# Linear attention in rounds of two pairs of chunks: both projections side by side, the transposes of one pair at the end of the round

## The chip, the cores and the metric

The kernel runs on one core of one Trainium2 chip. The metric is the device time of one execution in microseconds (us), from start to end. A core has five engines: TensorE (PE; its weight loads are listed apart as PEld), VectorE (DVE), ScalarE (ACT), GpSimd (POOL) and SyncE (SP). Each runs its own instructions in order, and waits by semaphores for the others and for transfers. PSUM, the memory that matmuls write, has eight banks; a tile below is one or two of them.

## The reference

Two layers follow one another. The first is linear attention for 8 batches, 8 heads, 576 tokens and 64 numbers per head; the second sends each of the 4608 tokens through one of eight experts.

```python
def phi(x):
    proj = x @ w_phi                                  # 64 -> 128 features
    proj = proj - max(abs(proj), axis=-1)
    return concat([exp(proj), exp(-proj)])            # 256 features
q_p, k_p = phi(q), phi(k)
kv  = einsum('bhsf,bhsd->bhfd', k_p, v)               # a sum over the 576 tokens
z   = k_p.sum(over tokens)
num = einsum('bhsf,bhfd->bhsd', q_p, kv)
den = einsum('bhsf,bhf->bhs', q_p, z) + 1e-06
x   = num / den                                       # 512 numbers per token over all heads
# second layer, per token
logits = x @ w_gate; local = sigmoid(x @ w_local)
e = argmax(logits) if s == 0 or local < 0.5 else the previous token's e
out = softmax(logits)[e] * (relu(x @ w1[e]) @ w2[e])
```

Everything is float32. The change concerns the first layer alone.

## The kernel before

**Units, chunks, pairs.** Two batches and two heads form a unit; there are 4 x 4 = 16 units. The 1152 tokens of the two batches are cut into nine chunks of 128, so chunk 4 holds the end of one batch and the start of the other. The 144 chunks are handled in 72 pairs. A unit has two halves: chunks 0 to 4 (the first batch) and 4 to 8 (the second), each with a sum of its own.

**What is done with a pair**, with the lines of the profile:
- *projections* (`proj`, L183): 8 matmuls, which the profile counts as 16 weight loads, into the tile "pj" (two banks; there are two such tiles). DVE reduces to the largest absolute value (m, L186) and subtracts (sb, L188). ACT takes exp of the keys, with both signs (kp, L192).
- *transposes* (`qtr`, L203): four, of the queries' part of sb, into "qt", a single bank. ACT takes exp out of it (qp, L206).
- *sums* (`kv`, L225): 8 matmuls a chunk (16 for chunk 4, which belongs to both halves) gather the sum over tokens of features by values in "kvp", a single bank. When a half is complete, ACT copies it out twice (kf and kvs, L244 and L245).
- *turn* (L251): one step after that, kf is transposed into one of the two banks named "nm", and ACT copies it out (ks, L254). *Gate logits* (L263): one step later still, ks times the router's weights goes to the end of the other "nm" bank, and ACT copies it into kvs (L265). From then on the half's outputs stand in a list, `todo`.
- *outputs* (L284): 8 entries of `todo` a chunk, one matmul (two weight loads) each, in groups of two or three chunks, into an "nm" bank. The first group of a half uses the bank in which its gate logits were formed; the second group takes the next bank of the two. At a group's end DVE reads it in four instructions: den + 1e-06 and its reciprocal (rc, L301, L302), the output (xo, L306) and the logits (lg, L308). Only then is the bank free.

**The steps.** `step(p)` issues on PE the projections of pair p, the transposes of pair p-1, turns and gates that are due, the sums of the two chunks of pair p-2 (KVLAG = 2) up to the end of a half, up to 18 entries of `todo` (QUOTA), the rest of the sums, and then the router's chores. PE's order is exactly as it is written; the order on DVE, ACT, POOL and SP is made by a scheduler from the dependences. Inputs are fetched in groups of three chunks, a few pairs ahead.

**The router's chores.** When four units with the same two batches are done, a generator (`gate`) finds each token's expert from the logits, ranks the tokens and writes lists. It advances by up to six yields a step. Its small matmuls (L432, L442, L455, L466) use the "qt" bank under the name "pt". Three of the four such gates run beside the attention. Some chores are paced by POOL: `paced` copies the latest m.

After the attention, from about 340 us on, the experts run; each weight is split into a high and a low part and each product is three matmuls (L799 to L801). That part isn't changed.

Of the kernel before, what the change touches and what calls it, by code (L numbers as in the profile page):

```python
# [6 lines left out]
F32 = mybir.dt.float32  # L7
# [22 lines left out]
WE, WR, WL = 8, 4, 1  # L30
FILL = 6
KVLAG = 2
QUOTA = 18

# [12 lines left out]
class Kernel:  # L47
# [9 lines left out]
    def run(self):  # L57
        nc, tc, A = self.nc, self.tc, self.A
        act, dve = self.act, self.dve
        with ExitStack() as root:  # L60
# [35 lines left out]
            self.scattering = False  # L96
            self.tail, self.eslots, self.scattered = False, [], []
            self.g, self.ch, self.kvb, self.lg = {}, {}, {}, {}
            n = NBP * NHP * NC
# [7 lines left out]
            with tc.manual_schedule(engines={mybir.EngineType.PE}):  # L107
                for p in range(n // 2):
                    while self.fetched < n // 3 and self.fetched * 3 < 2 * p + 8:
                        self.fetch_kqv(self.fetched)  # L110
                    if p == FILL:
# [3 lines left out]
                    self.step(p, n)  # L115
            self.tail = True
            p = n // 2
            while p < n // 2 + KVLAG + 1 or self.todo or self.turns or self.gates:
                self.step(p, n)
                p += 1  # L120
            for x in self.background:
# [5 lines left out]
            more = lambda: next(plan, None)  # L127
# [44 lines left out]
    def proj(self, p):  # L172
# [3 lines left out]
        t = self.psf.tile([128, 2, 2, 2, 128], F32, name="pj")  # L176
        for i in (2 * p, 2 * p + 1):
            kq = self.g[i // 3]["kq"]
            s = slice(i % 3 * 128, i % 3 * 128 + 128)
            for j in (0, 1):  # L180
                for h in (0, 1):
                    r = slice(64 * h, 64 * h + 64)
                    self.last_pe = self.pe.matmul(t[:, h, i % 2, j, :], kq[r, j, s], self.w2[r], start=True, stop=True)  # L183
        m = self.m = self.front3.tile([128, 8], F32, name="m")
        f = t.rearrange("p h c j f -> p (h c j) f")
# [161 lines left out]

    def step(self, p, n):

        if p < n // 2:  # L350
            self.proj(p)
        if 0 <= p - 1 < n // 2:
            self.qtr(p - 1)
        gates, self.gates = self.gates, []
        turns, self.turns = self.turns, []
        for x in turns:
            x()
        for x in gates:
            x()
        parts = [[]]  # L360
        if 0 <= p - KVLAG < n // 2:
            for i in (2 * (p - KVLAG), 2 * (p - KVLAG) + 1):
                a, *more = self.kv(i)
                parts[-1] += a
                parts += more
        for x in parts[0]:
            x()
        for _ in range(min(QUOTA, len(self.todo)) if p < n // 2 else len(self.todo)):
            self.todo.pop(0)()
        for part in parts[1:]:  # L370
            for x in part:
                x()
        for x in list(self.background):
            for _ in range(6):
                y = next(x, self)
                if y is self:
                    self.background.remove(x)
                if y is self or y is STEP:
                    break

    def paced(self):

# [4 lines left out]
        return self.tc.issue_after(self.pool.tensor_copy(t, self.m[:, 0:1]).ins)  # L387

# [619 lines left out]
```

## Time and profile before

| | us |
|---|---|
| three runs | 838.76, 828.74, 834.18 |
| median | 834.18 |
| profiled execution | 827.13 |
| its span | 825.4 |
| mean granted clock of PE | 0.995 |

The profiled execution is the fastest of the times shown; around its span lie 1.7 us. Busy shares of the engines over the span say little about one stage, since the attention (up to some 335 us) and the experts have different limits. So the stage is read by its own windows and by PE's weight loads in order of time. In those rows stand start, length, engine, line, operation, output and inputs, and a count; behind them in brackets idle time and what ended it. The shape before the type is that of the tile which is read.

### The profile page before, as it was taken

The page shows a single profiled execution, that of the slowest core. Times are in us where ns is not written, and L with a number is a line of the kernel's source. Part 1 is how long each engine was busy: PE and PEld are TensorE (multiplying, and loading weights), DVE is VectorE, ACT ScalarE, POOL GpSimd, SP SyncE. Part 2 cuts the span into 40 slices and gives each one's busy share as a digit, 9 for nine tenths or more (in the row PEclk, how much of TensorE's full clock was granted, in tenths as well). Part 3 has the DMA queues.
Part 4 walks back from the last instruction along what each step waited for, and adds up shares of the span by engine and source line. Part 5 has one row for each costly group of instructions (what it writes and reads, how often), then busy time and mean ns, then how long its engine had stood idle before and what let it go on. Part 6 is the DMA issues. An engine that isn't in the chain of part 4 may idle for free.

```text
span 825.4 us, 23470 instructions
## 1 busy us (share of the span) xinstructions
PE 788.1 (95%) x9777; PEld 710.0 (86%) x9777; DVE 555.4 (67%) x956; ACT 428.2 (52%) x738; POOL 146.7 (18%) x156
## 2 busy tenths in 40 slices
PE   6999998999989899888999999999999999999997
PEld 5899987898878788777898998998898898999896
DVE  5677897679878885848754444644686777568541
ACT  4666665566666565323543333533564557447431
POOL 0000002200231132051421202212122212201010
PEclk9999999999999999999999999999999999999999
DMA  6545546764799531574974433744696687767510
GB/s 193 141 123 135 144 130 92 124 149 126 151 215 236 168 102 36 157 138 136 393 255 141 162 116 121 286 141 148 207 346 211 209 319 263 257 224 273 192 44 23
DMA packets 74239, 145.01 MB, mean 176 GB/s; under 512 B 9198, under 2 KB 48757, under 8 KB 74112
## 3 DMA queue, kind: packets, MB, share of 16 engines
q1 hardware_dynamic: 66272, 123.14, 50.9%
q0 software_dynamic: 7792, 20.02, 7.2%
q8 instruction: 79, 1.29, 0.7%
q10 hardware_dynamic: 64, 0.30, 0.1%
q14 instruction: 32, 0.26, 0.1%
HBM read 124.51 MB, written 20.26 MB: 175 GB/s over the span
## 4 chain that ended last, share of the span: by engine, by line
PE 69%; issue 12%; DMA 7%; DVE 6%; ACT 2%; POOL 2%; another core or an unknown queue 1%; SPq 1%; POOLq 0%; DVEq 0%; ACTq 0%
PE l L799 12%; PE l L800 12%; PE l L801 12%; PE kvp L225 8%; PE pj L183 8%; PE nm L284 8%; PE qt L203 4%; DMA out<-y,p_tokm 4%; DMA wraw<-in_w2h 2%; PE tr L791 1%; DVE sb L188 1%; DVE m L186 1%; PE nm L263 1%; POOL out L874 1%; DMA p_lrm<-lst,p_rim 1%
## 5 line engine op out<-in xcount | busy, mean ns | idle before, releaser
L753 ACT CAST whi<-wraw 128x1024 fp32r<-128x1024 f32 x160 | 167.5, 1048 | 205.7 <-PE l L801 111.6
L754 DVE TENSOR_TENSOR wlo<-wraw,whi 128x1024 fp32r<-128x1024 f32 x160 | 195.7, 1224 | 85.9 <-ACT whi L753 83.6
L799 PE MATMUL l<-xhi,whi 128*128 128x256 f32 x544 | 155.2, 286 | 2.1 <-DVE hl L822 1.4
L800 PE MATMUL l<-xlo,whi 128*128 128x256 f32 x544 | 152.8, 281 | 0.3 <-DVE xlo L794 0.3
L801 PE MATMUL l<-xhi,wlo 128*128 128x256 f32 x544 | 152.4, 280 | 0.0
L799 PE MATMUL l<-whi,hh 128*128 128x512 f32 x320 | 127.4, 398 | 0.7 <-DVE y L873 0.7
L800 PE MATMUL l<-wlo,hh 128*128 128x512 f32 x320 | 125.8, 393 | 0.0
L801 PE MATMUL l<-whi,hl 128*128 128x512 f32 x320 | 125.7, 393 | 0.0
L186 DVE TENSOR_REDUCE m<-pj 128x8 f32<-128x1024 f32 x72 | 87.9, 1220 | 43.9 <-PE pj L183 43.7
L206 ACT ACTIVATE qp<-qt 128x512 f32<-128x512 f32 x144 | 84.7, 604 | 60.3 <-PE qt L203 57.9
L192 ACT ACTIVATE kp<-sb 128x512 f32<-128x512 f32 x144 | 82.9, 623 | 54.2 <-DVE sb L188 46.5
L799 PEld LDWEIGHTS l<-xhi,whi 128*128 128x128 f32 x544 | 102.8, 189 | 4.5 <-DVE hl L822 1.9
L800 PEld LDWEIGHTS l<-xlo,whi 128*128 128x128 f32 x544 | 102.8, 189 | 1.1 <-DVE xlo L794 0.5
L801 PEld LDWEIGHTS l<-xhi,wlo 128*128 128x128 f32 x544 | 102.9, 189 | 0.0
L284 PE MATMUL nm<-kvs,qp 128*64 128x74 f32 x2304 | 89.0, 230 | 6.8 <-ACT kvs L265 4.8
L183 PE MATMUL pj<-first,kq 64*128 64x128 f32 x1152 | 86.9, 291 | 8.1 <-DMA kq<-in_kqT 6.4
L874 POOL DMA_INDIRECT out<-y,p_tokm x34 | 44.4, 1305 | 269.2 <-DVE y L873 250.7
L188 DVE TENSOR_TENSOR sb<-pj,m 128x1024 f32<-128x1024 f32 x72 | 88.1, 1224 | 3.7
L284 PEld LDWEIGHTS nm<-kvs,qp 128*64 128x64 f32 x2304 | 81.2, 139 | 8.1 <-ACT kvs L265 5.3
L183 PEld LDWEIGHTS pj<-first,kq 64*128 64x128 f32 x1152 | 72.6, 193 | 13.9 <-issue 6.8
L225 PE MATMUL kvp<-v,kp 128*64 128x65 f32 x2048 | 78.1, 227 | 0.5 <-ACT kvs L245 0.4
L225 PEld LDWEIGHTS kvp<-v,kp 128*64 128x64 f32 x2048 | 68.5, 140 | 6.6 <-issue 5.4
(200 smaller groups left out, 1000.3 us busy)
## 6 DMA issues: line engine op xcount, KB each, us to landing
wraw<-in_w1h SPq DMA_DIRECT2D x80, 512.0 KB, 5.9
wraw<-in_w2h SPq DMA_DIRECT2D x80, 512.0 KB, 4.4
kq<-in_kqT SPq DMA_DIRECT2D x47, 384.0 KB, 4.6
v<-in_va SPq DMA_DIRECT2D x48, 195.0 KB, 3.0
xs<-xo SPq DMA_DIRECT2D x48, 128.0 KB, 4.1
xs<-xo SPq DMA_DIRECT2D x16, 192.0 KB, 2.1
vs<-in_va SPq DMA_DIRECT2D x32, 32.5 KB, 3.0
lst<-pr,ri POOLq DMA_INDIRECT x36, 6.3
```

The costliest lines, as they stand in the source:

```text
L183: self.last_pe = self.pe.matmul(t[:, h, i % 2, j, :], kq[r, j, s], self.w2[r], start=True, stop=True)
L186: dve.tensor_reduce(m, f, AX.X, ALU.max, apply_absolute_value=True)
L188: self.last_dve = dve.tensor_sub(sb.rearrange("p h c j f -> p (h c j) f"), f, m.unsqueeze(2).broadcast_to([128, 8, 128]))
L192: self.last_act = act.activation(kp[:, :, :, sg, :].rearrange("p c h f -> p h c f"), sb[:, :, :, 0], AF.Exp, scale=1.0 - 2 * sg)
L206: self.act.activation(qp[:, sg], t, AF.Exp, scale=1.0 - 2 * sg)
L225: self.pe.matmul(self.kvp[r, sg, h], self.ch[i]["kp"][:, h, sg, r], self.v(i, b)[:, h], start=first and n < 2, stop=last and n >= 6)
L284: self.pe.matmul(e["t"][r, c - c0, h, :], self.ch[i]["qp"][:, sg, h, q0 + r.start:q0 + r.stop], kvs[:, sg, h, :], start=sg == 0, stop=sg == 1)
L753: self.act.copy(hi, raw)
L754: self.dve.tensor_sub(lo, raw, hi.bitcast(F32))
L799: mm(o, ah, bh, start=first, stop=False)
L800: mm(o, ah, bl, start=False, stop=False)
L801: self.last_pe = mm(o, al, bh, start=False, stop=last)
```

## The change

The work is cut into 36 rounds of two pairs instead of 72 steps of one. Round i issues on PE:
1. the projections of pairs 2i and 2i+1, one behind the other;
2. the transposes of pair 2i-1;
3. turns and gates that are due, now counted in rounds: a turn one round after its half is complete, and the gate one round after that;
4. the sums of chunks 4i-4 to 4i-1 up to the end of a half, up to 32 entries of `todo` (before 18 a step, so 36 in two), and the rest of the sums;
5. half of the router's chores;
6. the transposes of pair 2i;
7. the other half of the chores.

Before, two steps held projections, transposes and outputs twice each in turn. The chores keep two advances per two pairs. kp gets five buffers instead of four. m of both pairs is kept for the pacing. The input groups are fetched as far ahead of the round's second pair as before.

```diff
-FILL = 6
-KVLAG = 2
-QUOTA = 18
+FILL = 3
+QUOTA = 32
...
-                for p in range(n // 2):
-                    while self.fetched < n // 3 and self.fetched * 3 < 2 * p + 8:
+                for i in range(n // 4):
+                    while self.fetched < n // 3 and self.fetched * 3 < 4 * i + 10:
                         self.fetch_kqv(self.fetched)
...
-            while p < n // 2 + KVLAG + 1 or self.todo or self.turns or self.gates:
+            while i < n // 4 + 2 or self.todo or self.turns or self.gates:
...
-        kp = self.front3.tile([128, 2, 2, 2, 128], F32, name="kp", bufs=4)
+        kp = self.front3.tile([128, 2, 2, 2, 128], F32, name="kp", bufs=5)
...
-    def step(self, p, n):
-
-        if p < n // 2:
-            self.proj(p)
-        if 0 <= p - 1 < n // 2:
-            self.qtr(p - 1)
+    def step(self, i, n):
+
+        last = n // 2
+        for p in (2 * i, 2 * i + 1):
+            if p < last:
+                self.proj(p)
+        if 0 <= 2 * i - 1 < last:
+            self.qtr(2 * i - 1)
         gates, self.gates = self.gates, []
         turns, self.turns = self.turns, []
...
         parts = [[]]
-        if 0 <= p - KVLAG < n // 2:
-            for i in (2 * (p - KVLAG), 2 * (p - KVLAG) + 1):
-                a, *more = self.kv(i)
+        for c in range(4 * i - 4, 4 * i):
+            if 0 <= c < n:
+                a, *more = self.kv(c)
                 parts[-1] += a
                 parts += more
         for x in parts[0]:
             x()
-        for _ in range(min(QUOTA, len(self.todo)) if p < n // 2 else len(self.todo)):
+        for _ in range(min(QUOTA, len(self.todo)) if i < n // 4 else len(self.todo)):
             self.todo.pop(0)()
         for part in parts[1:]:
             for x in part:
                 x()
+        self.chores(0)
+        if 2 * i < last:
+            self.qtr(2 * i)
+        self.chores(1)
+
+    def chores(self, k):
+        self.half = k
         for x in list(self.background):
```

The lines of the changed kernel are one lower than before from L183 to L308 (L284 becomes L283, L308 becomes L307) and eight higher from the chores on.

How the change moves instructions is shown at three places. In the rows, the number behind a name tells one tile of that name from another, and a semaphore that an instruction waits for is in brackets.

**PE, where outputs change from one group to the next.** Before, in a step with a turn (nm_1446), the group nm_1371 is finished and nm_1477 is begun:

```order
L203 MATMUL qt_1438<-first_62,sb_1358 128x128 x3
L251 MATMUL nm_1446<-first_62,kf_1393 128x128 [waits DVE_49,PE_49,Activation_49]
L251 MATMUL nm_1446<-first_62,kf_1393 128x128
L225 MATMUL kvp_1451<-v_1040,kp_1285 64x65 [waits DMAHW2_49,Activation_49]
L225 MATMUL kvp_1451<-v_1040,kp_1285 64x65 x15
L284 MATMUL nm_1371<-kvs_1238,qp_1063 64x74 x2
L284 MATMUL nm_1477<-kvs_1238,qp_1063 64x74 [waits Activation_49]
L284 MATMUL nm_1477<-kvs_1238,qp_1063 64x74 x7
L284 MATMUL nm_1477<-kvs_1238,qp_1146 64x74 x8
```

The new group takes the bank of the turn, which ACT's copy frees. Now, in round 10, turn and gate (nm_1414) stand in one round, and the group nm_1273 is finished behind four chunks of sums:

```order
L262 MATMUL nm_1414<-wgi_68,ks_1271 64x18 [waits Activation_49]
L262 MATMUL nm_1414<-wgi_68,ks_1271 64x18 x3
L224 MATMUL kvp_1420<-v_919,kp_1241 64x65 [waits DMAHW0_49]
L224 MATMUL kvp_1420<-v_919,kp_1241 64x65 x15
L224 MATMUL kvp_1420<-v_919,kp_1257 64x65 x8
L224 MATMUL kvp_1420<-v_1065,kp_1257 64x65 [waits DMAHW2_49]
L224 MATMUL kvp_1420<-v_1065,kp_1257 64x65 x7
L283 MATMUL nm_1273<-kvs_997,qp_914 64x74 x8
L283 MATMUL nm_1468<-kvs_997,qp_914 64x74 [waits DVE_49,PE_49]
L283 MATMUL nm_1468<-kvs_997,qp_914 64x74 x7
L283 MATMUL nm_1468<-kvs_997,qp_958 64x74 x8
L283 MATMUL nm_1414<-kvs_1153,qp_958 64x74 [waits Activation_49]
```

The gate has the bank of the turn, and the group nm_1468 takes that of nm_1273, so its first output waits for DVE.

**DVE, at the same two places.** Before, the four instructions on the finished group nm_1371 stand behind reduce and subtract of the step's one pair:

```order
L186 TENSOR_REDUCE m_1431<-pj_1422 128x8 [waits PE_49]
L188 TENSOR_TENSOR sb_1433<-pj_1422,m_1431 128x1024 [waits DVE_49,Activation_49]
L301 TENSOR_SCALAR rc_1470<-nm_1371 128x4 [waits PE_49,Activation_49]
L302 RECIPROCAL rc_1470<-rc_1470 128x4 [waits DVE_49]
L306 TENSOR_TENSOR xo_1473<-nm_1371,rc_1470 128x256 [waits DMAHW6_49,DVE_49]
L308 TENSOR_TENSOR lg_430<-nm_1371,rc_1470 128x2x2x9
```

Now those on nm_1273 stand behind reduce and subtract of both pairs of round 10:

```order
L185 TENSOR_REDUCE m_1378<-pj_1369 128x8 [waits PE_49]
L187 TENSOR_TENSOR sb_1380<-pj_1369,m_1378 128x1024 [waits DVE_49,Activation_49]
L185 TENSOR_REDUCE m_1394<-pj_1385 128x8 [waits PE_49]
L187 TENSOR_TENSOR sb_1396<-pj_1385,m_1394 128x1024 [waits DVE_49,Activation_49]
L300 TENSOR_SCALAR rc_1461<-nm_1273 128x6 [waits PE_49]
L301 RECIPROCAL rc_1461<-rc_1461 128x6 [waits DVE_49]
L305 TENSOR_TENSOR xo_1464<-nm_1273,rc_1461 128x384 [waits DMAHW4_49,DVE_49]
L307 TENSOR_TENSOR lg_554<-nm_1273,rc_1461 128x3x2x9
```

Two more large instructions stand ahead of them within the round.

**ACT, at the end of a half.** Before, the two copies out of the sums' bank (kf_1393, kvs_1394) stand ahead of the exponentials of the keys of that step:

```order
L265 COPY kvs_1238<-nm_1371 128x4x9
L206 ACTIVATE qp_1368<-qt_1363 128x512
L244 COPY kf_1393<-kvp_1259 128x256
L245 COPY kvs_1394<-kvp_1259 128x4x65
L192 ACTIVATE kp_1360<-sb_1358 128x2x2x128 x2
L206 ACTIVATE qp_1443<-qt_1438 128x512
```

Now, in round 16, the second copy (kvs_2414) stands behind the exponentials of the first pair (kp_2351) and one of those of the second (kp_2367):

```order
L253 COPY ks_2381<-nm_2378 128x256
L191 ACTIVATE kp_2351<-sb_2349 128x2x2x128
L264 COPY kvs_2039<-nm_2383 128x4x9
L191 ACTIVATE kp_2351<-sb_2349 128x2x2x128
L243 COPY kf_2413<-kvp_2269 128x256
L205 ACTIVATE qp_2375<-qt_2370 128x512
L191 ACTIVATE kp_2367<-sb_2365 128x2x2x128
L244 COPY kvs_2414<-kvp_2269 128x4x65
L191 ACTIVATE kp_2367<-sb_2365 128x2x2x128
```

The copy has moved behind work on the round's second pair.

More of the change, by code (lines that the diff above doesn't have):

```diff
@@ L96, in run @@
             self.scattering = False
-            self.tail, self.eslots, self.scattered = False, [], []
+            self.tail, self.eslots, self.scattered, self.m = False, [], [], [None, None]
             self.g, self.ch, self.kvb, self.lg = {}, {}, {}, {}
@@ L386, in paced @@
         t = self.small.tile([128, 1], F32, name="tick", bufs=2)
-        return self.tc.issue_after(self.pool.tensor_copy(t, self.m[:, 0:1]).ins)
+        return self.tc.issue_after(self.pool.tensor_copy(t, self.m[self.half][:, 0:1]).ins)
     def pst(self, shape):
```

12 lines of the change are left out of this document (6 added, 6 removed).

## Prediction

> **What bounds the kernel now.** I read the page first: the busy rows, the chain of waits by engine, and the costliest groups.
>
> ```profile
> span 825.4 us, 23470 instructions
> PE 788.1 (95%) x9777; PEld 710.0 (86%) x9777; DVE 555.4 (67%) x956; ACT 428.2 (52%) x738; POOL 146.7 (18%) x156
> PE 69%; issue 12%; DMA 7%; DVE 6%; ACT 2%; POOL 2%; another core or an unknown queue 1%; SPq 1%; POOLq 0%; DVEq 0%; ACTq 0%
> L186 DVE TENSOR_REDUCE m<-pj 128x8 f32<-128x1024 f32 x72 | 87.9, 1220 | 43.9 <-PE pj L183 43.7
> L188 DVE TENSOR_TENSOR sb<-pj,m 128x1024 f32<-128x1024 f32 x72 | 88.1, 1224 | 3.7
> L183 PEld LDWEIGHTS pj<-first,kq 64*128 64x128 f32 x1152 | 72.6, 193 | 13.9 <-issue 6.8
> ```
>
> PE ends the kernel nearly alone, so an edit is worth what it takes from or adds to PE's row of work. The change touches only the attention stage, so I read it by windows next (us; busy and count of PE, PEld, DVE, ACT, POOL; granted clock).
>
> ```profile
> 50.00:100.00 50.00, 50.00 (x1126) 45.34 (x1122) 38.53 (x69) 31.44 (x70) 0.00 (x0) 1.00 0.48 131
> 250.00:300.00 50.00, 46.12 (x996) 41.47 (x992) 42.64 (x101) 30.99 (x64) 9.28 (x14) 0.99 0.72 194
> ```
>
> Between 50 and 100 us PE has no gap at all, while DVE is busy 38.53 of 50, 77%. Whatever makes PE wait is lost in full. Later, with the router's work beside it, PE is idle for 3.9 of 50 us.
>
> Then I read the weight loads on PE in order of time, since their starts give the pitch of the steps (start, length, instruction):
>
> ```profile
> 34.76 0.97 PEld L183 LDWEIGHTS pj<-first,kq 64*128 64x128 f32 x16
> ...
> 37.60 1.23 PEld L284 LDWEIGHTS nm<-kvs,qp 128*64 128x64 f32 x36
> 38.75 0.56 PEld L225 LDWEIGHTS kvp<-vs,kp 128*64 128x64 f32 x16
> ...
> 54.64 1.23 PEld L284 LDWEIGHTS nm<-kvs,qp 128*64 128x64 f32 x36
> 55.95 0.97 PEld L183 LDWEIGHTS pj<-first,kq 64*128 64x128 f32 x16
> 57.04 0.42 PEld L203 LDWEIGHTS qt<-first,sb 128*128 128x128 f32 x4
> 57.63 0.55 PEld L225 LDWEIGHTS kvp<-vs,kp 128*64 128x64 f32 x16 [0.17 <-issue]
> ...
> 59.42 0.55 PEld L225 LDWEIGHTS kvp<-vs,kp 128*64 128x64 f32 x16
> 59.88 0.55 PEld L225 LDWEIGHTS kvp<-v,kp 128*64 128x64 f32 x16
> ...
> 94.20 0.42 PEld L203 LDWEIGHTS qt<-first,sb 128*128 128x128 f32 x4
> ...
> 321.82 0.42 PEld L203 LDWEIGHTS qt<-first,sb 128*128 128x128 f32 x4
> ```
>
> From the transposes at 57.04 to those at 94.20 stand 9 undisturbed steps: 37.16 us, 4.13 each. 34.76 is where the projections of pair 8 start (the first of what will be round 4) and 321.82 where the transposes of the last pair stand: 287.1 us for 64 steps. At the undisturbed pitch they would take 64/9 x 37.16 = 264.2, so 22.9 us of the stage are disturbances already.
>
> **The change, part by part.** The sum is made against the profiled execution, 827.1 us, the fastest shown; the median of the three runs is 834.2, 0.9% above, and the range has to carry that.
>
> *Fewer changes of kind on PE.* Sixteen projection loads of 193 ns end 0.97 after the first start, so one follows the other by (0.97 - 0.193)/15 = 0.052, and sixteen take 0.83; but the transposes start 1.09 after the projections. The change of kind costs 0.26. From outputs to sums it is 1.15 for 36 loads (37.60 to 38.75), from outputs to projections 1.31 (54.64 to 55.95): 0.16. From transposes to the next kind it is 0.59 (57.04 to 57.63), of which some 0.20 belong to the change. Two steps hold 2 x (0.26 + 0.20 + 0.16) = 1.24; a round holds one each of projections to transposes, transposes to sums, outputs to transposes and transposes to projections, about 0.82. It saves **0.42 a round**. Nine rounds take 2 x 37.16 - 9 x 0.42 = 70.5 us, 7.83 each, and rounds 4 to 35 take 250.7. The Trainium skill ("TensorEngine Tiling (Array Packing)", Key Properties) says that a change of tiling mode drains TensorE; the rows agree with 0.16 to 0.26 each, and by that rule alone the change could only gain.
>
> *A new wait for a bank.* This is the term that decides. The outputs, the turn and the gate logits share two PSUM banks. Before, a turn and a gate never stand in one step, since they alternate. Now the turn of one half of a unit and the gate of the half before it come in the same round. Where a round begins with a group of outputs half done, that group holds one bank; the turn takes the other and the gate takes it after the turn; so the next group of outputs must have the bank of the group just finished, and that is free only after DVE's four instructions (1/den, two products) have read it. The order of PE shows it: the first output of the second group waits for DVE. Of such outputs the order has 24 after the change and 9 before. And on DVE these four now stand behind reduce and subtract of *both* pairs:
>
> ```profile
> 98.88 1.23 DVE L186 TENSOR_REDUCE m<-pj 128x8 f32<-128x1024 f32 x1 [0.95 <-PE pj L183]
> 100.14 1.23 DVE L188 TENSOR_TENSOR sb<-pj,m 128x1024 f32<-128x1024 f32 x1
> ...
> 122.58 0.15 DVE L301 TENSOR_SCALAR rc<-nm 128x4 f32<-128x4 f32 x1
> 122.76 0.18 DVE L302 RECIPROCAL rc<-rc 128x4 f32<-128x4 f32 x1
> 122.98 0.42 DVE L306 TENSOR_TENSOR xo<-nm,rc 128x256 f32<-128x256 f32 x1
> 123.32 0.22 DVE L308 TENSOR_TENSOR lg<-nm,rc 128x36 f32<-128x36 f32 x1
> ...
> 298.48 0.97 PEld L183 LDWEIGHTS pj<-first,kq 64*128 64x128 f32 x16
> 299.76 1.23 DVE L186 TENSOR_REDUCE m<-pj 128x8 f32<-128x1024 f32 x1 [1.25 <-PE pj L183]
> ```
>
> The first reduce starts 1.28 after the round's first projection (298.48 to 299.76). Reduce and subtract follow at 1.26 (98.88 to 100.14), so the fourth of them ends at 1.28 + 4 x 1.26 = 6.32; the four instructions take 122.58 to 123.54, 0.96, and the bank is free 7.28 us after the round's start (7.43 with three chunks in the group, as an estimate). PE reaches the output sooner: two projections, transposes, turn, gate and up to four chunks of sums are 1.9 + 0.4 + 0.4 + 0.2 + 1.9 = 4.8, and the rest of the first group little more. Behind the waiting output stand the round's other outputs (0.064 each, 1.15 / 18), what is left of the sums (0.058 each, 0.46 / 8 from 59.42 to 59.88), and the transposes of the even pair with their change of kind (0.16 + 0.59 = 0.75). With r outputs and k sums left, the round lasts **7.28 + 0.064 r + 0.058 k + 0.75**, instead of 7.83 on average.
>
> Walking the order, I find twenty such rounds from round 4 on:
> - 10, 19, 28: r about 23, k 0: 9.65 (three-chunk group), sum 28.9
> - 11, 20, 29: r 23, k 32: 11.36, sum 34.1
> - 6, 15, 24, 33: r 6.5, k 16: 9.37, sum 37.5
> - 14, 23, 32: r 6, k 16: 9.34, sum 28.0
> - 17, 26, 35: r 30, k 8: 10.56 (three-chunk), sum 31.7
> - 18, 27: r 30, k 0: 9.95, sum 19.9
> - 22, 31: r 13, k 24: 10.25, sum 20.5
>
> Together 200.6, against 20 x 7.83 = 156.6: **+44**. Its bounds: nothing, if the four instructions were ready sooner; 44 if all bind. The trace of before has this wait once, where a turn needed the bank:
>
> ```profile
> PE nm L251 <- DVE lg L308: 1.7, 1, 1.7
> ```
>
> So it is real where it binds, and I take the 44.
>
> *ACT in five other rounds.* In rounds 7, 8, 16, 25 and 34 the copy of a finished sum out of its only bank (L244) stands on ACT behind exponentials of the second pair, which wait for the second subtract at 6.32. The next sum needs that bank. The durations:
>
> ```profile
> 122.02 0.38 ACT L245 COPY kvs<-kvp 128x260 f32<-128x260 f32 x1
> 298.61 1.15 ACT L192 ACTIVATE kp<-sb 128x512 f32<-128x512 f32 x2 [1.31 <-DVE sb L188]
> 300.27 1.09 ACT L206 ACTIVATE qp<-qt 128x512 f32<-128x512 f32 x2 [0.51 <-PE qt L203]
> ```
>
> The bank is free at 6.32 + 0.58 (one of the two exponentials) + 0.38 = 7.3, and with 8 to 24 sums (0.5 to 1.4) and the 0.75 behind it the round lasts 8.5 to 9.4, instead of 7.83: 0.7 to 1.6 more, five times 3.5 to 8. The bounds are 0, if the exponentials were done before, and 10, with both exponentials ahead; I take **+7**.
>
> *The router's chores around the even transposes.* They use the one bank of the transposes ("pt" beside "qt"). Before, a chore stood between outputs and projections, and the next transposes came 1.1 later; now it stands directly ahead of, or behind, the even transposes.
>
> ```profile
> 109.33 0.09 PEld L432 LDWEIGHTS pt<-first,g_code 128*9 128x9 f32 x1
> 109.95 0.27 DVE L434 COPY g_cr<-pt 9x128 f32<-9x128 f32 x1
> ```
>
> The tile at 109.33 was read until 110.22, 0.9 later; transposes right behind wait for that, and a chore right behind transposes waits for their exponentials (0.51 + 1.09 on ACT). I count four or five such places in each of the three gates that run beside the attention, 0.6 to 1.5 each: **+13**, bounds 0 and 20. DMA issues are moved with their steps, the fetches keep their distance in pairs, and SP and POOL do not end PE's waits in the undisturbed window, so I cost them at nothing; if a fetch came late, its price is the projections' row of waits, some 2 us each.
>
> *What recurs.* Of the 22.9 us of disturbances (the router and the first expert weights beside the stage, as in the window from 250) about half have nothing to do with the order and come again: **+11**, bounds 0 and 23. *Ends.* The first four rounds do 37 outputs fewer (131 instead of 94 are left at the end, by the order): -2.4, and 1.1 of changes of kind: **-3.5**. The tail gets the 2.4, one more pair of transposes (0.6) and turn and gate one behind the other, with about 3 us of waits: **+6**.
>
> *The clock.* After an idle stretch the granted clock fell: outputs that take 1.23 took 2.27.
>
> ```profile
> 145.38 2.27 PEld L284 LDWEIGHTS nm<-kvs,qp 128*64 128x64 f32 x36 [3.74 <-ACT kvs L265]
> 145.00:147.00 2.00, 1.61 (x26) 1.62 (x28) 0.00 (x0) 1.86 (x6) 0.00 (x0) 0.57 1.09 200
> 246.16 0.74 PEld L183 LDWEIGHTS pj<-first,kq 64*128 64x128 f32 x10 [1.88 <-issue]
> 248.00:249.00 1.00, 1.00 (x20) 1.00 (x22) 1.00 (x2) 1.00 (x3) 0.45 (x1) 0.50 0.44 95
> 273.29 0.20 PEld L251 LDWEIGHTS nm<-first,kf 128*128 128x128 f32 x2 [1.86 <-issue]
> ```
>
> It fell after 3.74 us, and after 1.88 at 246; after 1.86 at 273 it did not. The new waits are 1.3 to 3.5 us long, so a few will do it: **+2**, with +30 if all twenty did (1.5 each). The Trainium skill ("TensorE: Matmul & The Clock Gate", What's actually happening) gives half clock after an idle window of about 3.4 us. The 3.74 agrees and the 1.88 differs; by the rule only rounds 11, 20 and 29 are at risk, some 5 us.
>
> *Sum.* 250.7 + 44 + 7 + 13 + 11 = 325.7 for rounds 4 to 35, against 287.1: +38.6. With -3.5, +6 and +2: +43. 827.1 + 43 = **870**.
>
> **Rivals.**
> 1. *Only the changes of kind count.* The bank comes free before PE asks for it, and 32 x 0.42 = 13.4 us are gained: 814. For it: the view of what PE waits for has, between 20 and 322 us, no output (L284) that waits for DVE, though 9 could by the order. Against it: the order of DVE, where both subtracts stand ahead; it decides from the point at which the four instructions end before 5 us in the round. 0.05.
> 2. *Waits and gain cancel*: the wait binds in only six or seven rounds, 6.5 x 2.2 = 14: 827 to 835. 0.05.
> 3. *The new waits swallow the old ones.* While PE waits, DVE and ACT catch up, and chores and disturbances (13 + 11) fall into the same gaps: 846, between 838 and 855. For it: DVE has 23% idle in the undisturbed window. 0.15.
> 4. *The clock follows the waits down* in most rounds: 870 + 10 to 30, 880 to 900. For it the 1.88 at 246, against it the 1.86 at 273. 0.12.
>
> That the change doesn't do what it says is excluded by the order: PE has the two projections side by side in every round.
>
> **How the numbers follow.** The forecast, 855 to 890, gets the remaining 0.63. About 1% is what a measurement of this kernel tells from no change (the runs of before spread by 1.2%). Faster by over 1%: rival 1, 0.05. Within 1%: rival 2, 0.05. Slower by over 1%: 0.90. The range 846 to 896 holds the forecast, half of rival 3 and most of 4: 0.8. Its low end is rival 3's time, or a bank term of 20 instead of 44; its high end is 870 with chores and disturbances at their upper bounds (+7, +12) and the median's 7 us above the profiled execution.
>
> **What would show it.** Right: PE's waits in the profile after have outputs (L283) waiting for DVE's last product (L307), some twenty times, 40 us and more together; rounds of the kinds above last 9.3 to 11.4 between their first projections; DVE's reduce has less idle time ahead in pairs; projections to transposes still cost 1.09, but half as often. Wrong: if PE is as gapless from 50 to 100 us as before, the bank does not bind and rival 1 or 2 holds; if the granted clock is under 0.9 in many windows, rival 4. The prediction would fail above all if the scheduled order let the outputs wait less than 1 us, since DVE's 7.28 rests on its row of four being gapless and PE's 4.8 on no wait of its own.

## Result: 6.7% slower, and the profile after

| | before | after |
|---|---|---|
| runs | 838.76, 828.74, 834.18, 830.92 | 882.68, 884.75, 883.87, 891.09 |
| median | 832.55 | 884.31 |
| span of the profiled execution | 825.4 | 880.9 |
| mean granted clock of PE | 0.995 | 0.98 |

The ratio is 1.0666 (95% interval 1.0624 to 1.0708). Run once more in a later series, beside before at 823.9, it was 1.0703 (1.0656 to 1.0750).

The page after has, in the places that were read before:

```profile
span 880.9 us, 23444 instructions
PE 790.0 (90%) x9777; PEld 714.5 (81%) x9777; DVE 559.1 (63%) x956; ACT 427.6 (49%) x738; POOL 142.8 (16%) x153
PE 53%; DVE 18%; issue 13%; DMA 8%; ACT 4%; POOL 3%; SPq 1%; POOLq 0%; DVEq 0%; ACTq 0%
L283 PE MATMUL nm<-kvs,qp 128*64 128x74 f32 x2304 | 91.7, 236 | 31.7 <-DVE lg L307 22.7
```

PE has the same 9777 instructions and nearly the same busy time, so nearly all of the 55.5 us are waiting. DVE went from 6% to 18% of the chain, and outputs wait for its last product. The windows of the stage (us; busy and count of PE, PEld, DVE, ACT, POOL; clock):

```profile
50.00:100.00 50.00, 43.99 (x996) 40.13 (x992) 36.56 (x61) 29.76 (x67) 0.00 (x0) 1.00 0.45 125
250.00:300.00 50.00, 39.38 (x869) 36.25 (x870) 38.07 (x78) 28.27 (x58) 10.22 (x17) 0.93 0.67 190
```

The stretch that had no gap before has 6.0 us of them now. The view of what PE waits for, from 20 to 390 us (us in total, times, longest):

```profile
PE nm L283 <- DVE lg L307: 22.7, 13, 4.0
PE nm L262 <- ACT ks L253: 11.0, 22, 0.7
PE kvp L224 <- ACT kvs L244: 5.8, 7, 1.8
PE nm L283 <- DVE rc L300: 5.5, 7, 1.4
PE pt L450 <- ACT qp L205: 3.5, 3, 1.2
PE pt L474 <- ACT qp L205: 3.5, 3, 1.2
...
PE qt L202 <- ACT qp L205: 1.3, 2, 1.0
PE nm L283 <- DVE rc L301: 1.2, 1, 1.2
PE qt L202 <- DVE g_cr L442: 1.1, 3, 0.4
```

Outputs waiting for DVE are 22.7 + 5.5 + 1.2 = 29.4 us. In time, 28.2 of them are twenty waits, one in each of the twenty rounds that the prediction lists from 6 to 35; the last, 1.2, stands at 367.96, behind the rounds. The starts of rounds show what they cost (weight loads of PE; 76.62 is round 9, 94.34 round 11):

```profile
76.62 1.86 PEld L182 LDWEIGHTS pj<-first,kq 64*128 64x128 f32 x32 [0.17 <-issue]
84.30 1.86 PEld L182 LDWEIGHTS pj<-first,kq 64*128 64x128 f32 x32 [0.17 <-issue]
94.34 1.86 PEld L182 LDWEIGHTS pj<-first,kq 64*128 64x128 f32 x32 [0.17 <-issue]
106.95 1.86 PEld L182 LDWEIGHTS pj<-first,kq 64*128 64x128 f32 x32 [0.17 <-issue]
114.39 1.86 PEld L182 LDWEIGHTS pj<-first,kq 64*128 64x128 f32 x32 [0.17 <-issue]
```

Round 9, without the wait, lasts 7.68, round 10 10.04, round 11 12.61, round 12 again 7.44.

Where the 55.5 us of span lie, by four points in both traces: the start of round 4 (34.76 before, 33.74 after), the start of the transposes behind the last round (321.82; after 358.56, where the transposes of the second last pair end), the first expert matmul (337.9; 381.5), and the end. Rounds 4 to 35 take 287.1 and 324.8, +37.7; the start -1.0; the tail 16.1 and 22.9, +6.8; what is behind the first expert matmul 487.5 and 499.4, +11.9. The last was not foreseen. It is one wait, shown by what PE waits for between 375 and 460 us and by POOL's order in time, after:

```profile
PE pt L585 <- DMA p_lrf<-lst,p_rif: 10.9, 1, 10.9
```

```profile
354.22 0.98 POOL L518 DMA_INDIRECT lst<-pr,ri  x1 [0.16 <-issue]
392.38 0.95 POOL L518 DMA_INDIRECT lst<-pr,ri  x1 [37.18 <-DVE ri L488]
...
403.73 0.96 POOL L518 DMA_INDIRECT lst<-pr,ri  x1 [0.30 <-issue]
410.03 0.89 POOL L573 DMA_INDIRECT p_lrf<-lst,p_rif  x1 [5.34 <-DMA lst<-pr,ri]
412.44 0.99 POOL L518 DMA_INDIRECT lst<-pr,ri  x1 [1.52 <-DMA p_lrf<-lst,p_rif]
```

The third gate writes its lists in nine transfers, one advance of the chores at a time. When the rounds end, eight are issued, the last at 354.22. The read of these lists (p_lrf) and the ninth write come behind the nine writes of the fourth gate, and the read has landed only at 412. (The ninth write stands even behind the read, for whose landing the row of 412.44 waits; so the read is made before that write.) Before, the ninth write was issued at 320.51 and the read at 325.40:

```profile
320.51 0.98 POOL L510 DMA_INDIRECT lst<-pr,ri  x1 [0.48 <-DMA lst<-pr,ri]
325.40 0.89 POOL L565 DMA_INDIRECT p_lrf<-lst,p_rif  x1 [3.92 <-DMA lst<-pr,ri]
```

### The profile page after: what moved, and what is told of

Same layout as the page of the kernel before. It is cut to its first block, busy times and chain, and to the rows that moved or that the text cites. A ratio compares the mean times of both kernels' runs of the same rounds, so it can differ in the third digit from the quotient of the medians.

```text
span 880.9 us, 23444 instructions
## 1 busy us (share of the span) xinstructions
PE 790.0 (90%) x9777; PEld 714.5 (81%) x9777; DVE 559.1 (63%) x956; ACT 427.6 (49%) x738; POOL 142.8 (16%) x153
## 4 chain that ended last, share of the span: by engine, by line
PE 53%; DVE 18%; issue 13%; DMA 8%; ACT 4%; POOL 3%; SPq 1%; POOLq 0%; DVEq 0%; ACTq 0%
PE l L807 11%; PE l L808 11%; PE l L809 11%; DVE m L185 6%; DVE sb L187 6%; PE nm L283 5%; PE pj L182 5%; PE kvp L224 5%; DMA out<-y,p_tokm 4%; PE qt L202 3%; DMA wraw<-in_w1h 2%; ACT kp L191 1%; ACT qp L205 1%; DMA wraw<-in_w2h 1%; DVE wlo L762 1%
## 5 line engine op out<-in xcount | busy, mean ns | idle before, releaser
L809 PE MATMUL l<-xhi,wlo 128*128 128x256 f32 x544 | 152.5, 280 | 0.0
L809 PE MATMUL l<-whi,hl 128*128 128x512 f32 x320 | 126.5, 395 | 0.6 <-DVE hl L830 0.6
L185 DVE TENSOR_REDUCE m<-pj 128x8 f32<-128x1024 f32 x72 | 87.7, 1218 | 55.8 <-PE pj L182 55.6
L283 PE MATMUL nm<-kvs,qp 128*64 128x74 f32 x2304 | 91.7, 236 | 31.7 <-DVE lg L307 22.7
L205 ACT ACTIVATE qp<-qt 128x512 f32<-128x512 f32 x144 | 80.6, 596 | 67.7 <-PE qt L202 67.0
L283 PEld LDWEIGHTS nm<-kvs,qp 128*64 128x64 f32 x2304 | 85.0, 143 | 34.9 <-issue 29.2
L191 ACT ACTIVATE kp<-sb 128x512 f32<-128x512 f32 x144 | 86.8, 630 | 39.4 <-DVE sb L187 37.1
L809 PEld LDWEIGHTS l<-xhi,wlo 128*128 128x128 f32 x544 | 103.0, 189 | 0.0
L182 PE MATMUL pj<-first,kq 64*128 64x128 f32 x1152 | 79.4, 291 | 6.5 <-DMA kq<-in_kqT 6.5
L224 PE MATMUL kvp<-v,kp 128*64 128x65 f32 x2048 | 72.3, 224 | 2.4 <-ACT kvs L244 2.4
L807 PEld LDWEIGHTS l<-whi,hh 128*128 128x128 f32 x320 | 60.6, 189 | 15.4 <-DVE y L881 2.5
```

What stands on the lines that cost most here:

```text
L185: dve.tensor_reduce(m, f, AX.X, ALU.max, apply_absolute_value=True)
L191: self.last_act = act.activation(kp[:, :, :, sg, :].rearrange("p c h f -> p h c f"), sb[:, :, :, 0], AF.Exp, scale=1.0 - 2 * sg)
L205: self.act.activation(qp[:, sg], t, AF.Exp, scale=1.0 - 2 * sg)
L224: self.pe.matmul(self.kvp[r, sg, h], self.ch[i]["kp"][:, h, sg, r], self.v(i, b)[:, h], start=first and n < 2, stop=last and n >= 6)
L283: self.pe.matmul(e["t"][r, c - c0, h, :], self.ch[i]["qp"][:, sg, h, q0 + r.start:q0 + r.stop], kvs[:, sg, h, :], start=sg == 0, stop=sg == 1)
L807: mm(o, ah, bh, start=first, stop=False)
```

## Experiments

Ratios below are to before in the same series. The theory is the prediction's: the bank of a half-finished group is handed over by DVE behind both pairs. The rivals are that rounds of two pairs are slow whatever the banks do, and that other waits hold the time.

**Quota 40 instead of 32.**

```diff
-QUOTA = 32
+QUOTA = 40
```

> The changed kernel with QUOTA 40 instead of 32: a round now issues all outputs that are due (a half of a unit brings 32 or 40), so none begins with a half-finished group, and turn and gate find both banks in turn. In PE's order 5 outputs wait for DVE instead of 24. Theory (the bank of an unfinished group, freed by DVE behind both pairs, is the loss): the waits of outputs for DVE, 29 us in the trace, fall under 5, the last lists are written before the attention ends, so the wait of 10.9 us for them goes too; time 884 - 44 - 11 = about 829, between 815 and 840. Rival A (rounds of two pairs are slow in themselves, because DVE and ACT do their work in larger lumps): 865 to 880. Rival B (only the late lists go): 873.

Measured: 1.0144 (1.0095 to 1.0192), median 835.3 beside 824.3. In its view of PE's waits, outputs no longer wait for DVE at all (a turn and a gate still do, 1.4 and 1.3), the gate waits for the turn's copy 0.5 us instead of 11.0, the wait for the lists is gone, and what leads is this:

```profile
PE kvp L224 <- ACT kvs L244: 10.1, 5, 3.4
...
PE pt L450 <- ACT qp L205: 3.5, 3, 1.2
PE pt L474 <- ACT qp L205: 3.5, 3, 1.2
```

It is the one number that brings back most of the loss: 1.0703 - 1.0144 = 5.6% or 46 us, about the sum of the three waits that are gone (29.4 + 10.5 + 10.1, the last from the repeat of the change below) less the 4.3 by which the wait for the copy of the sums (L244) has grown. Rivals A and B fall. In the profiled execution, the fastest of the four, the first expert matmul comes at 338.1, as before the change (337.9). In a later series it was again run as a reference:

> Quota 40 once more, beside the next: 1.014 of before in every theory.

There it was 1.0203 (1.0155 to 1.0250); the intervals overlap, and by this figure 41 us are brought back. The first profile has a granted clock of 0.991 and the second 0.979; in the second the first expert matmul comes only at 354.8, and from 270 to 300 and 300 to 330 us the granted clock is 0.83 and 0.89, where the first has 1.00 in both. So 338.1 is the good case, and 1.4 to 2.0% stay lost.

**Quota 36, twice the quota before.**

```diff
-QUOTA = 32
+QUOTA = 36
```

> The changed kernel with QUOTA 36, twice the 18 of the kernel before. It tells whether the loss is only that the change lowered the quota of two pairs from 36 to 32. In PE's order 16 outputs wait for DVE (24 at 32, 5 at 40), and the third gate's lists are written ahead of the fourth's. Theory (each such wait costs 1.3 to 2.5 us and drags a gate behind the turn's copy; lists 10 us): between the two, 1.030 to 1.045 of before. Rival (the quota of 32 alone is at fault, and 36 does as well as before): 1.00 to 1.015. Rival (any limit that leaves an unfinished group costs the same): 1.05 to 1.06.

Measured: 1.0252 (1.0207 to 1.0296), a little under the stated span and well over its first rival. So the larger part of the loss, over 4 of the 6.7 to 7.0%, came with the smaller quota of two pairs (32 for 36), but not all of it: with 36 the changed kernel is still 2.5% slower than before, where quota 40, in the same series, is 2.0% slower. Outputs still wait for DVE, 3.0 us in six places, and gates 8.5 in twelve. No run has the kernel before with a quota of 16 a step, so what so low a quota costs without the rounds stays open. In the nine rounds from 4 to 12, ahead of the router's work, the time by the starts of the rounds is 79.2 (quota 32, in the repeat), 75.9 (36) and 73.1 (40); eighteen steps before take 74.3 at the undisturbed pitch.

**Quota 40 without the change.**

```diff
-QUOTA = 18
+QUOTA = 40
```

> The kernel before with QUOTA 40 instead of 18: each step issues all outputs that are due. It tells whether a high quota helps by itself, without the change. Theory (before, unfinished groups seldom wait for a bank, since turn and gate never share a step): within 1% of before, 825 to 840. Rival (leftover outputs cost before as well): 815 to 823.

Measured: 1.0054 (1.0030 to 1.0078). A high quota doesn't help the kernel before; it takes away something that only the change brings.

**The second projection at the round's end.**

```diff
-        for p in (2 * i, 2 * i + 1):
-            if p < last:
-                self.proj(p)
+        if 2 * i < last:
+            self.proj(2 * i)
...
         self.chores(0)
         if 2 * i < last:
+            self.proj(2 * i + 1)
             self.qtr(2 * i)
```

> The changed kernel with the second projection of a round moved from its start to its end, ahead of the even transposes; quota, turns, gates and chores as in the change. So the projections are apart again as before the change, while the rest of the round stays. Reduce and subtract of the second pair now run across the round's border, and the bank of a finished group is free about 5.4 us after the start instead of 7.3. Theory (place of the second pair on DVE sets the length of the wait): the twenty rounds lose 23 us instead of 44, the change of kind that is saved (0.26 a round, 8 us) is lost again: 884 - 21 + 8 = about 871. Rival A (the wait comes from quota and banks whatever DVE does first): 892. Rival B (the side by side projections are the whole loss): 835 to 845.

Measured: 1.0882 (1.0839 to 1.0926), slower than the change. As a time it agrees with rival A (892 against 897.9), but its waits say why it is slow, and that is another thing:

```profile
PE qt L202 <- DVE sb L187: 30.7, 27, 1.9
PE nm L283 <- DVE lg L307: 15.5, 10, 2.6
PE nm L262 <- ACT ks L253: 10.7, 22, 0.5
PE pt L585 <- DMA p_lrf<-lst,p_rif: 9.6, 1, 9.6
```

The pair projected at a round's end is due for its transposes 1.1 us after the next round's start (behind one projection), before DVE has subtracted; 30.7 us of new waits hide what was to be seen. The waits of outputs for DVE did fall to 17.5 (15.5 and two smaller rows of 1.4 and 0.6), from 21 to twelve, and most that are left last 1.2 to 1.4.

**A short reduce.** The largest value is taken from 16 of the 128 features, so the outputs are others; PE's order isn't changed.

```diff
-        dve.tensor_reduce(m, f, AX.X, ALU.max, apply_absolute_value=True)
+        dve.tensor_reduce(m, f[:, :, 0:16], AX.X, ALU.max, apply_absolute_value=True)
```

> The changed kernel with DVE's reduce over 16 of the 128 features only (the largest value is taken from fewer, so the outputs differ), about 0.25 us instead of 1.22; nothing else is changed, and PE's order is the same with its 24 outputs that wait for DVE. Theory (the bank is free when DVE has gone through reduce and subtract of both pairs and the four instructions): it comes free at 7.28 - 2 x 1.0 = 5.3 us after the start of the round, little later than PE asks, so the waits of outputs for DVE fall from 29 us to under 8, and the time by 35 to 45 us against the change, to 1.015 to 1.025 of before. The late lists (11 us) and the chores (12 us) stay. Rival A (the round's loss has to do with PE's order, the banks and ACT, whatever DVE does): less than 10 us gained. Rival B (DVE's whole work is the bound): 72 us less, about before or faster.

Measured: 1.0920 (1.0875 to 1.0964). The whole time can't be used, since other outputs give other routes: the second layer runs one more unit, as the count of its matmuls shows beside the repeat of the change.

```profile
L807 PEld LDWEIGHTS l<-whi,hh x320: 186/188/330, 393.9 to 868.8; 128*128 128x128 f32 x160
```

```profile
L807 PEld LDWEIGHTS l<-whi,hh x328: 186/188/330, 397.8 to 887.4; 128*128 128x128 f32 x164
```

(The first fence is the repeat, the second the short reduce.) The attention can be read apart from it: the first expert matmul comes at 382.9, beside 380.3. So nothing was gained there either, and the prediction of 35 to 45 us failed. PE's waits show that it was moved:

```profile
PE nm L262 <- ACT ks L253: 30.0, 22, 2.5
PE nm L283 <- DVE lg L307: 16.7, 12, 3.1
```

Outputs wait for DVE 17.9 us instead of 29.3 (22.9 + 5.2 + 1.2 in the repeat), less, but not under 8. Where no gate waits ahead, in rounds 11, 20 and 29, the theory is met: the output starts 5.37, 5.44 and 5.30 after the round's first projection, for which 5.3 was expected, instead of 7.04, 7.12 and 8.17 in the repeat, and waits 1.2 to 1.4 instead of 3.0 to 4.0. Round 11, which starts at 96.47:

```profile
101.84 1.76 PE L283 MATMUL nm<-kvs,qp 128*64 128x74 f32 x48 [1.36 <-DVE lg L307]
```

The late second projection had moved it in the same way, to 5.56 and 5.64 in rounds 11 and 20 (6.66 in 29), where 5.4 was expected. So the place of the four instructions on DVE does set when the bank comes free. But the gates now wait 30.0 instead of 11.0. In round 10, ACT has both exponentials of the keys ahead of the turn's copy (start, length, instruction; PE's gate behind):

```profile
88.50 1.15 ACT L191 ACTIVATE kp<-sb 128x512 f32<-128x512 f32 x2 [1.67 <-DVE sb L187]
89.55 0.35 ACT L253 COPY ks<-nm 128x256 f32<-128x256 f32 x1
89.96 0.41 PE L262 MATMUL nm<-wgi,ks 128*64 128x18 f32 x8 [1.47 <-ACT ks L253]
```

A faster DVE makes these exponentials ready sooner, and they take the place of the copy for which PE waits. The control:

> The control for the last one: the kernel before with the same shortened reduce. All theories that call the loss a new wait: 0 to 8 us less than before, since DVE stands hidden there. If DVE bounds both kernels alike, it gains as much as in the changed kernel.

Measured: 1.0156 (1.0104 to 1.0207), with the same additional unit in the second layer, so the time doesn't tell what the attention gained. In the trace the first expert matmul comes at 334.6, beside 337.9 before: 3.3 us, within the 0 to 8 expected, though this is one reading and the profiled execution, 846.2, the slowest of its four.

**Lists early.**

```diff
         self.chores(1)
+        if i >= 27:
+            self.chores(1)
```

> The changed kernel with one more advance of the router's chores in each round from 27 on, so that the third gate writes its lists before the attention ends, as it did before the change. Theory (11 us of the loss are one wait of PE for the lists of the third gate, whose ninth write and whose read now stand on POOL behind the nine writes of the fourth): 873, and PE no longer waits for p_lrf. Rival (the wait covers work that is late anyway, such as weights): 880 to 885.

Measured: 1.0636 (1.0590 to 1.0682), beside 1.0666 and 1.0703. The wait for p_lrf is gone: from the first expert matmul to the last one that begins a group (L809, x544) it is 387.9 to 847.4, 459.5, where the change has 469.7. But that first matmul comes 6.4 later than in the profile of the change (381.5). Of this, 1.9 lie ahead of round 27 (it starts at 260.64 instead of 258.74), where nothing is changed yet. The other 4.5 are in part additional chores at the transposes' bank: from round 27 on, four of them (L465, L587, L442, L597) wait 1.2 each for the exponentials, where the change has two such waits; the rest isn't traced to a wait. So the wait for the lists is real, and this way of removing it costs some half of it again.

**Chores elsewhere, with quota 40.**

```diff
         for x in parts[0]:
             x()
+        self.chores(0)
...
-        self.chores(0)
+        self.chores(1)
         if 2 * i < last:
             self.qtr(2 * i)
-        self.chores(1)
```

> Quota 40 as in the first experiment, and the chores moved: half of them between sums and outputs, half ahead of the even transposes, so that none stands right behind transposes whose bank ACT has still to read. Theory (the chores around the even transposes are what is left of the loss, 4.1 us per gate and three gates): 8 to 12 us less than with quota 40 alone, so 0.995 to 1.005 of before. Rival (the rest is ACT's late copies of sums): 0 to 3 us less, 1.01 of before.

Measured: 1.0214 (1.0159 to 1.0270), not better than quota 40 alone (1.0144 and 1.0203). A chore behind the sums waits for the odd transposes' exponentials about as long (6.7 us in all for L450 and L474, beside 7.0):

```profile
122.97 0.09 PEld L450 LDWEIGHTS pt<-g_dg,consts 9*9 9x9 f32 x2 [1.65 <-ACT qp L205]
```

**Odd transposes behind the sums, with quota 40.**

```diff
-        if 0 <= 2 * i - 1 < last:
-            self.qtr(2 * i - 1)
+        self.chores(1)
         gates, self.gates = self.gates, []
...
         for x in parts[0]:
             x()
+        if 0 <= 2 * i - 1 < last:
+            self.qtr(2 * i - 1)
...
             self.qtr(2 * i)
-        self.chores(1)
```

> Quota 40, the transposes of the odd pair moved behind the sums, and the second half of the chores moved between the two projections and the turn. A chore then finds its bank long read (projections, 1.9 us, cover the exponentials of the even pair), the odd transposes stand 2.7 us behind it, and the next chore stands behind all outputs. Theory (PE's waits of chores for qp, 7.0 us with quota 40, and a part of the 3.3 us of transposes for qp are what is left to remove): 7 to 10 us less than quota 40 alone, 1.002 to 1.007 of before; together with the saved changes of kind perhaps level with it. Rival (as with the chores behind the sums: the wait only changes its place, since ACT has the exponentials of the keys ahead): 1.012 to 1.022.

Measured: 1.0306 (1.0270 to 1.0343). The chores' waits for qp are gone, but those of the transposes rise from 2.0 in the quota 40 of this series to 6.7. Round 13, the first with a chore on that bank, lasts 9.09 instead of 10.17. But every undisturbed round lasts 8.45 instead of 8.15, as the same place of the two kernels shows, quota 40 alone first:

```profile
53.51 0.55 PEld L224 LDWEIGHTS kvp<-vs,kp 128*64 128x64 f32 x16
53.98 2.13 PEld L283 LDWEIGHTS nm<-kvs,qp 128*64 128x64 f32 x64
```

```profile
56.35 0.55 PEld L224 LDWEIGHTS kvp<-vs,kp 128*64 128x64 f32 x16
56.97 0.42 PEld L202 LDWEIGHTS qt<-first,sb 128*128 128x128 f32 x4
57.56 2.12 PEld L283 LDWEIGHTS nm<-kvs,qp 128*64 128x64 f32 x64 [0.17 <-issue]
```

From sums to outputs it was 0.47; with transposes between it is 1.21, 0.74 for four loads, which at the start of the round had cost 0.39 (51.54 to 51.93). A fifth change of kind costs about 0.3 a round, 10 us in 36.

**Even transposes ahead of the outputs, with quota 40.**

```diff
         for x in parts[0]:
             x()
+        if 2 * i < last:
+            self.qtr(2 * i)
...
+            if k == 24:
+                self.chores(0)
             self.todo.pop(0)()
+        if k < 24:
+            self.chores(0)
...
-        self.chores(0)
-        if 2 * i < last:
-            self.qtr(2 * i)
         self.chores(1)
```

> Quota 40, the transposes of the even pair moved ahead of the outputs (behind the first part of the sums), the first half of the chores between the 24th and 25th output, the second at the end of the round. The number of changes of kind per round stays four (sums to transposes and transposes to outputs in place of outputs to transposes and transposes to projections), unlike the run before, where it rose to five and cost 0.30 a round. A chore finds the even transposes read by ACT during the outputs, and the projections of the next round cover its own reading. Theory: PE's waits of chores for qp (7.0 us) and of transposes for a chore's reading (2 us) go, clean rounds keep 8.15: 1.005 to 1.012 of before. Rival (stalls only change place, as in the last two attempts): 1.015 to 1.03.

Measured: 1.0612 (1.0561 to 1.0662), and neither the theory nor the rival holds. Its view of PE's waits begins with

```profile
PE qt L202 <- ACT qp L205: 44.0, 33, 3.4
```

The even transposes need the bank of the odd ones, whose second exponential stands on ACT behind those of the keys. The repeat of the change itself, the reference for three of these runs:

> The changed kernel once more, beside the next three, since chips differ by some 1% (before: 832.5 and 824.3 on two occasions). Every theory: 1.067 of before.

Its ratio stands at the top. No version tried beats before.

## Why the prediction was right, and where it was not

The time (884.3, forecast 870, range 846 to 896) came out as forecast, and the bank as its main cause; by the steps:

*Changes of kind, 0.42 a round.* Right. Rounds without waits last 8.14 where a chunk 4 brings 80 loads of sums (round 4) and 7.68 where there are 64 (5 and 9); nine rounds hold four of the first kind, and 4 x 8.14 + 5 x 7.68 = 71.0, a little less for a turn and a gate that are missing once each (12, 21 and 30, without the gate, last 7.44). The prediction worked out 70.5, and eighteen steps before take 74.3. With quota 40, nine rounds take 73.1, of which about 2 are stall in one round that has no outputs to issue. The price of one change is shown from the other side too, by the fifth one: 0.30. The rule of the Trainium skill that a change of tiling mode drains TensorE ("TensorEngine Tiling (Array Packing)", Key Properties) agrees; by it alone the time would have been 814.

*The bank, +44.* The mechanism is shown: twenty waits in the twenty rounds of the list, the two runs that move DVE's work and the output with it, and the quota that ends the waits and brings back 41 to 46 us together with the lists and the gates' waits. The size is shown by the rounds. In eighteen of the twenty the waiting output starts 7.04 to 7.77 after the round's first projection (8.17 in 29, 9.25 in 31), for which the prediction had 7.28 and 7.43. Rounds 6, 17, 18, 19, 22 and 28, without waits of chores, last 9.35, 10.64, 10.06, 9.85, 10.34 and 9.77; its formula gives 9.37, 10.56, 9.95, 9.65, 10.25 and 9.65. Rounds 10 and 27 are 0.4 and 0.5 longer than it gives, and 11, 20 and 29, where the clock fell too, 1.3 to 3.2. In eighteen rounds DVE comes to the four instructions without a gap. In 11, 20 and 29 it even has the second subtract between the first two of them; the first projection of round 11 stands at 94.34:

```profile
99.34 1.22 DVE L187 TENSOR_TENSOR sb<-pj,m 128x1024 f32<-128x1024 f32 x1
100.48 0.17 DVE L301 RECIPROCAL rc<-rc 128x4 f32<-128x4 f32 x1
100.68 0.42 DVE L305 TENSOR_TENSOR xo<-nm,rc 128x256 f32<-128x256 f32 x1
101.02 0.21 DVE L307 TENSOR_TENSOR lg<-nm,rc 128x36 f32<-128x36 f32 x1
```

```profile
101.38 3.19 PE L283 MATMUL nm<-kvs,qp 128*64 128x74 f32 x48 [3.03 <-DVE lg L307]
```

The next group starts at 101.38, 7.04 after the round's start. In rounds 10 and 28 it is otherwise: PE itself was late, by the gate's wait, and DVE waited for PE, in round 10 by 0.25.

```profile
90.77 0.17 DVE L300 TENSOR_SCALAR rc<-nm 128x6 f32<-128x6 f32 x1 [0.25 <-PE nm L283]
```

```profile
92.06 1.76 PE L283 MATMUL nm<-kvs,qp 128*64 128x74 f32 x48 [1.34 <-DVE lg L307]
```

There 1.34 us is the bare hand-over of a bank from PE to DVE and back, which no order of DVE removes where the group that gives the bank has only just ended; the short reduce and the late second projection leave waits of 1.2 to 1.4 too. Where that group ended earlier, the wait is shorter (0.2 to 0.8 in rounds 6, 14, 15, 23, 24, 32 and 33).

Two signs that the prediction named aren't met. Outputs wait 28.2 us in the rounds, not 40 and more: PE comes to them 5.8 to 7.0 us into most of these rounds, not at the 4.8 worked out (4.0 to 4.2 in 11, 20 and 29). A part of this is a wait that the prediction saw in the order and didn't price: in seventeen of the twenty rounds the gate has waited 0.5 to 0.7 for ACT's copy of the turn, 8.4 in all. Where DVE sets the start of the output, that wait adds nothing and only takes its time from the later one. And DVE's reduces have more idle time ahead of them than before, 55.8 us instead of 43.9; from round 4 on, all of it stands ahead of the first reduce of a round.

*ACT in five other rounds, +7.* The number agrees, but by luck. The twelve rounds without a wait for DVE, from 4 on, take 100.9 together, 6.9 over 12 x 7.83. But PE's wait for the copy (L244) in rounds 7, 8, 16, 25 and 34 is 0.2, 0.5, 0, 0.4 and 0.3: 1.4 us, where 3.5 to 8 were worked out. The rest of the 6.9 is made of other things: 0.5 to 0.7 of the gate's wait in four of these rounds, 1.5 of half clock in round 34, and 1.1 of the same copy in round 13, which the prediction didn't list.

*Chores +13 and recurring disturbances +11.* The twenty rounds take 223.9 instead of 200.6, 23.3 over, near the 24 of these two terms; but some 4 of them are the clock (below), so that this is in part luck. Of this 8.9 are waits around the even transposes by name (3.5 + 3.5 + 1.1 and 0.8 for another chore). With quota 40 the two rounds with chores (13 and 14) last 10.17 and 10.33 beside 8.15, 4.2 per gate, so 13 for three gates is about right. How the rest is shared between weights, DVE and clock stays open.

*Rounds 4 to 35* come out at 324.8, for which the sum was 325.7. So near a hit is partly luck, since errors in ACT's part, the disturbances and the clock make up for one another. *Start -3.5* was -1.0, and *tail +6* was +6.8.

*The clock, +2.* In rounds 11, 20 and 29, 44 to 48 matmuls of outputs took 2.9 to 3.2 us instead of 1.76 (the row of 101.38 above beside that of 92.06), after idle stretches of 3.0, 3.0 and 4.0: some 4 us. In round 34 the projections' loads took 3.35 instead of 1.86, at a granted clock of 0.50, behind waits of 1.2 at most. So +2 was low, and the loss in all is open. The Trainium skill ("TensorE: Matmul & The Clock Gate", What's actually happening) has half clock after an idle window of about 3.4 us. By it just rounds 11, 20 and 29 were at risk. Round 29 agrees; 3.0 in 11 and 20 and 1.2 ahead of 34 differ. And in the repeat of the change, 3.04 in round 11 was not followed by half clock (granted clock 1.00 from 100 to 104): the round lasts 11.18 there, near the 11.36 worked out, instead of 12.61.

*What failed* is a step that the prediction made in one sentence: SP and POOL were costed at nothing. POOL's share of the changed order was not followed past the end of the rounds. The third gate comes later beside the rounds: its first list write is issued 13.4 us before their end (345.17 and 358.56), where it was 25.4 (296.41 and 321.82). By the order this is due to the outputs that are left over, and with quota 36 or 40 the wait for the lists is gone. So the rounds end before its ninth list write, and the read waits behind the fourth gate's writes: 10.9 of the 12.7 us that 870 lacked (the profiled execution was 882.7).

## What to carry to other kernels

Where two stages share few PSUM banks, count who holds a bank at the start of each round: a group left unfinished by a quota turns a free bank into a hand-over through another engine, here 0.2 to 4.0 us each time, and some 1.3 where the group has only just ended and DVE has nothing else ahead. When an order is changed, follow each engine past the end of the changed loop, since work that is advanced one piece a round can miss its place there. A wait that is removed is worth what the next one in line leaves: five of these runs traded one wait for another at the same bank or engine.

## Not expected

Making DVE faster didn't help the attention: a reduce cut to an eighth of its features left it at 382.9 beside 380.3 us, since ACT's exponentials came earlier and were taken ahead of a copy of 0.35 us for which PE then waited (11.0 to 30.0 us). And a quota over what is produced on average (40, where a round brings 32 and a step of before 16) costs the kernel before 0.5%, but is worth about 5% with the change.
